# Urgent K and V of two input blocks, one VectorE key tile in the first run, and a stricter limit for TensorE's filling work

## The chip, the cores and the metric

The kernel runs on one core of a Trainium2 chip. The metric is the device time of one execution in microseconds (us). Single executions of one and the same kernel lie up to 10 us apart here, so most comparisons below rest on five or more executions a kernel, taken in three batches, each on one chip in turn with the kernel before, and name the mean granted clock of TensorE (PE).

## The reference

```python
def reference(A_x, A_wqkv, A_wo, B_x, B_w1, B_b1, B_w2, B_b2, c, w_mod):
    # x is 1 x 2048 x 512, 32 heads of 16, F = 1376, all bf16
    mod = (silu(c) @ w_mod).reshape(1, 6, 1, 512)       # sa, ca, ga, sb, cb, gb
    h = layernorm(x) * (1 + ca) + sa
    q, k, v = split_heads(h @ wqkv)
    x = x + ga * (merge(softmax(q @ k.T * 16 ** -0.5) @ v) @ wo)
    h = layernorm(x) * (1 + cb) + sb
    return x + gb * (gelu(h @ w1 + b1) @ w2 + b2)
```

## The kernel before: the parts that matter

The program is written by a list scheduler that runs when the kernel is built. Every operation is an object with an engine, an assumed duration, dependencies and a priority; the scheduler keeps a clock for each engine and emits the instructions in the order that it arrives at. The order is fixed from then on. On the chip each engine works its list in order and waits on semaphores.

The work is cut into 32 runs of 512 queries and four heads. A run has 16 key tiles of 128 keys, and a key tile has four units of 128x512 scores. ScalarE turns units into exp, two or three in an instruction. VectorE takes some key tiles with an integer form of exp: one conversion a unit, then four shifted copies a key tile. All products with V of one run add up in one accumulator, `od`, which has a single buffer and is copied to SBUF when the run ends. That copy, "the first OD copy", marks the end of run 0 below.

```python
OVER = 0.1                        # how much later than an exp's need a filler may end
HEAT = 1.3                        # us of PE work in 3.4 us below which passes of zeros are filled in
...
DKS = (2, 6, 10, 14)              # key tiles of a run that VectorE may take
FIRST_D, D_TIME = 1, 8.0          # from run 1 on
own = [[kt for kt in range(NT) if r < FIRST_D or kt not in DKS] for r in range(NR)]
shared = [[kt for kt in DKS if r >= FIRST_D] for r in range(NR)]
...
def ahead(self, can):             # what PE may start now
    q = [(s, o) for s, o in can if o.kind == "qkA"]
    if not q:
        return can
    limit = max(q[0][0], self.need() - q[0][1].us - PEL - 0.02) + OVER
    keep = []
    for s, o in can:
        end = s + o.us + (0.107 if o.mode[0] != "qk" else 0.0)
        if o.kind == "qkA" or end <= limit:
            keep.append((s, o))
    return keep
...
for b in range(NQ):               # the four input blocks: LN, transpose, modulate, Q, K, V
    kind = f"in{b}"
    if b < 2:
        urgent.add(kind)
    ... layer_norm(..., ("DVE", "DVE", "ACT", "ACT"), ...)
    make_k(b, 0, kind, r_ax, "ACT")
    make_v(b, 0, kind, ...)
...
    while ended:                  # when a run has ended
        ...
        urgent.add("in3")
```

The softmax here doesn't subtract the row's maximum and nothing guards it: scores larger than these inputs give would overflow.

Of the kernel before, what the change touches and what calls it, by code (L numbers as in the profile page):

```python
# [11 lines left out]
ACT = mybir.ActivationFunctionType  # L12
ALU = mybir.AluOpType
# [38 lines left out]

WIN = 3.4
PEL = 0.24
OVER = 0.1
DVE_PE = 0.0
DL = 0.14
DPL = 0.08
# [45 lines left out]
class Plan:  # L104
# [51 lines left out]
    def ahead(self, can):  # L156
# [6 lines that stand above are left out]
# [88 lines left out]
def kernel(  # L251
# [14 lines left out]
    nc = tc.nc  # L266
    P = 128
# [4 lines left out]
    NT = S // P  # L272
    QB = 512
    NQ = S // QB
    TPB = QB // P
# [6 lines left out]
    DKS = (2, 6, 10, 14)  # L282
# [4 lines left out]
    POOL_US, POOL_MIN = 0.68, 0.5  # L287
    A_US = {1: 0.49, 2: 0.92, 3: 1.345}
    PSUM_F = 4
    FIRST_D, D_TIME = 1, 8.0  # L290

    psum = bass.MemoryType.PSUM
    const = ctx.enter_context(tc.tile_pool(name="const", bufs=1))
# [7 lines left out]
    def res(name, n, shape, dt, pool=work):  # L301
        return Res(name, n, lambda i: pool.tile(shape, dt, name=f"{name}{i}"))
# [3 lines left out]
    r_st = [res(f"st{n}", 1, [P, n * QB], FP32, ps) for n in SPAN]  # L306
    r_od = res("od", 1, [P, QB], FP32, pp)
    r_ax = res("ax", 2, [P, QB], FP32, pp)
# [27 lines left out]
    urgent = set()  # L336
# [38 lines left out]
    def op(eng, *a, **k):  # L375
        o = Op(eng, *a, **k)
        if eng == "PE":
            o.due = due_now[0]
            due_now[0] += due_now[1]
        return plan.add(o)  # L380
# [30 lines left out]
    def free(owner, deps):  # L411
        return op("POOL", None, 0.0, deps, lat=0.0, prio=0.0, rel=(owner,))
# [38 lines left out]
    qmask = const.tile([P, 2], FP32, name="qmask")  # L451
# [55 lines left out]
    o_mask = op("DVE", mask, 0.4, (o_io,), prio=0.0)  # L507
# [129 lines left out]
    o_k = {}  # L637
# [5 lines left out]
    def proj(b, w, cc, kind, acq, after=None):  # L643
        return chain([(lambda ps, j=j: nc.tensor.matmul(  # L644
            out=ps[:, 0:QB], lhsT=w.tile[:, j, cc * P:(cc + 1) * P], rhs=o_h[b].tile[:, j, :],
            start=(j == 0), stop=(j == NC - 1)), MM) for j in range(NC)],
            [w, after] + o_hd[b], kind, acq, (o_h[b], w))

    def make_k(b, cc, kind, acq, eng):
        mm = proj(b, o_w[1], cc, kind, acq)  # L650
        o_k[(cc, b)] = op(eng, lambda o: copy(eng, kT[cc][b], mm.tile[:, 0:QB]), 0.6 if eng == 'DVE' else 0.5, (mm,), prio=0.3,
                          rel=(mm,))

    def make_q(b, cc, kind, acq):
        qm = op("POOL", None, 0.0, (), lat=0.0, prio=0.0, acq=r_qm)
        mm = proj(b, o_w[0], cc, kind, acq, after=qm)
        ev = op("DVE", lambda o: nc.vector.tensor_tensor(
            out=qm.tile, in0=mm.tile[:, 0:QB].unsqueeze(1).to_broadcast([P, 2, QB]),
            in1=qmask.unsqueeze(2).to_broadcast([P, 2, QB]), op=ALU.mult), 1.14, (mm, qm, o_mask),
            prio=0.3, rel=(mm,))  # L660
        evs = [ev, ev]
        o_q[(cc, b)] = (qm, evs)
        qm.uses += 1
        q_left[(cc, b)] = 8 * NT

    def make_v(b, cc, kind, acq, eng):
        def vt(ps, t):
            for j in range(NC):
                nc.tensor.matmul(out=ps[:, t * P:(t + 1) * P],  # L669
                                 lhsT=o_h[b].tile[:, j, t * P:(t + 1) * P],  # L670
                                 rhs=o_w[2].tile[:, j, cc * P:(cc + 1) * P],
                                 start=(j == 0), stop=(j == NC - 1))
        mm = chain([(lambda ps, t=t: vt(ps, t), 4 * 0.071) for t in range(TPB)],
                   [o_w[2]] + o_hd[b], kind, acq, (o_h[b], o_w[2]))

        def ev(o):
            dst = VEB[b][:, :, 8 * cc * VW:8 * (cc + 1) * VW].rearrange(
                "p t (h w) -> p t h w", w=VW)
            copy(eng, dst[:, :, :, 0:16], mm.tile[:, 0:QB].rearrange("p (t h d) -> p t h d", t=TPB, h=8))
        got = [op(eng, ev, 0.6, (mm, o_v0[b]), prio=0.3, rel=(mm,))]  # L680
        for t in DKS:
            if t // TPB == b:
                def scale(o, t=t):
                    for ph in range(1, NPH):
                        nc.gpsimd.tensor_scalar(  # L685
                            out=v_cols(VX[(t, ph)])[:, 8 * cc:8 * cc + 8, 0:16],
                            in0=v_cols(v_tile(t, 0))[:, 8 * cc:8 * cc + 8, 0:16], scalar1=PH_W[ph],
                            scalar2=0.0, op0=ALU.mult, op1=ALU.add)
                got.append(op("POOL", scale, 4 * 0.3, (got[0], o_v0[b]), prio=1.0, port=True))
        o_v[(cc, b)] = got  # L690
# [6 lines left out]
    NR = len(runs)  # L697
# [3 lines left out]
    def run_heads(r):  # L701
        b, u = runs[r]
        return (u % NC, None, u // NC) if b == LAST else (u // 2, u % 2, None)



    own = [[kt for kt in range(NT) if r < FIRST_D or kt not in DKS] for r in range(NR)]
    shared = [[kt for kt in DKS if r >= FIRST_D] for r in range(NR)]
    at = {"A": [0, 0, 3], "D": [0, 0, []]}
    turn = [0]  # L710

# [42 lines left out]
    def qk_deps(r, kt):  # L754
        want_q(r // 2 + 1 if r < LAST * 8 else r - LAST * 4 + 2)
        cc, par, hb = run_heads(r)
        qm, evs = o_q[(cc, runs[r][0])]
        return [evs[0], o_k[(cc, kt // TPB)]], qm

    def qk_a():  # L760
        got = []
# [16 lines left out]
        for r, kt, i in got:  # L778
            d, qm = qk_deps(r, kt)
            deps += d  # L780
            if qm not in rel:
                rel.append(qm)
# [28 lines left out]
    def qk_d():  # L811
# [10 lines left out]
        ph = o_ph[0]  # L822
        live["D"] += 1
        deps, qm = qk_deps(r, kt)
        last = len(rows) == 1

# [423 lines left out]
    prev_tr = after = None  # L1250
    for b in range(NQ):
        kind = f"in{b}"
        if b < 2:
            urgent.add(kind)
        o_h[b], o_hd[b], za, trs = layer_norm(
            lambda t, b=b: o_x[b].tile[:, t, :], o_x0 if b == 0 else [o_x[b]] * TPB, modA, o_mA, prev_tr, r_blk,
            ("DVE", "DVE", "ACT", "ACT"), tuple(r_st) if b == 0 else (r_ax, r_ax), kind, 0.6 + 0.2 * b, after)
        prev_tr = trs[-1]
        after = za[-1]
        o_h[b].uses += 1  # L1260
        free(o_x[b], za)
        if b == 0:
            make_q(0, 0, kind, r_st[0])
        make_k(b, 0, kind, r_ax, "ACT")
        make_v(b, 0, kind, r_st[1] if b == 0 else r_ax, "DVE")
# [14 lines left out]
    def want_q(g):  # L1280
        while q_made[0] < g and q_made[0] + 1 < NQ * NC:
            q_made[0] += 1
            b, cc = divmod(q_made[0], NC)
            due(32 + APR * (first_run(q_made[0]) - 1) - 32)
            make_q(b, cc, f"q{q_made[0]}", r_ax)
            due(1e9)
            if cc == NC - 1:
                o_h[b].uses -= 1
                if b == NQ - 1:
                    o_w[0].uses -= 1  # L1290
# [4 lines left out]
    while True:  # L1295
# [7 lines left out]
        while ended:  # L1303
            r = ended.pop(0)
            if r < NR - 1:
                normalise(r)
            b, u = runs[r]
# [72 lines left out]
```

## Time and profile before

| | kernel before |
|---|---|
| median of 3 executions | 813.59 us (811.69 to 815.46) |
| span of the profiled execution | 810.6 us |
| mean granted clock in it | 0.984 |
| ScalarE, VectorE, PE busy | 769.6, 737.2, 749.0 us |
| first exp, first OD copy, end of the last exp | 17.99, 60.56, 785.27 us |

An L with a number is a line of the program (from L662 on, the changed kernel's numbers are 4 higher, from L1255 on 3). In a line of the timeline, the first number is the start, the second the time to the end of the last of xN instructions, and the brackets hold the engine's idle time ahead of it and what ended that. In a line of the busy time in stretches, each engine has its busy time and, in brackets, its instructions; then come the granted clock, the share of the DMA engines and GB/s. The lines themselves stand in the prediction.

### The profile page before, as it was taken

What the parts mean: (1) busy time and instruction counts of PE and PEld (TensorE: products, weight loads), DVE (VectorE), ACT (ScalarE), POOL (GpSimd) and SP (SyncE); (2) the same over time, 40 slices, a digit from 0 to 9 for tenths busy, and PEclk for the clock granted to TensorE, in tenths of its full rate; (3) what the DMA queues carried; (4) which work ended last, traced back from release to release, by engine and by line L of the source; (5) the groups of instructions that cost most, each with busy time, mean ns of one, the idle gap of its engine ahead of it and who ended that gap; (6) DMA issues with size and microseconds to landing.
All of it is one profiled execution on the core that took longest, in us unless ns stands there. A gap on an engine that the chain in (4) does not pass through costs nothing. (4 is left out here: it accounts for less than half of the span.)

```text
span 810.6 us, 20166 instructions
## 1 busy us (share of the span) xinstructions
PE 749.0 (92%) x8217; PEld 280.3 (35%) x8217; DVE 737.2 (91%) x1281; ACT 769.6 (95%) x694; POOL 96.7 (12%) x241
## 2 busy tenths in 40 slices
PE   7889999999989999989999889989999999999997
PEld 3433333332223223223223223323234444444454
DVE  7728997989999999997899999999999999989994
ACT  2899999999999999999999999999999999999994
POOL 5321302100001100000001100000000110101100
PEclk8999999999999999989999999999999999999999
DMA  6304000002100000001110000000011001000010
GB/s 208 105 1 125 28 18 16 20 27 70 40 19 15 16 18 15 13 8 30 32 39 12 22 6 16 18 16 21 29 38 19 17 18 43 18 22 25 18 43 27
DMA packets 34199, 26.22 MB, mean 32 GB/s; under 512 B 15005, under 2 KB 29502, under 8 KB 34106
## 3 DMA queue, kind: packets, MB, share of 16 engines
q1 hardware_dynamic: 33578, 24.94, 11.0%
q8 instruction: 64, 1.05, 0.6%
q14 instruction: 29, 0.24, 0.1%
q10 hardware_dynamic: 528, 0.00, 0.0%
HBM read 21.30 MB, written 2.61 MB: 29 GB/s over the span
## 5 line engine op out<-in xcount | busy, mean ns | idle before, releaser
L798 ACT ACTIVATE pt<-st 128x1536 bf16<-128x1536 f32 x635 | 725.1, 1282 | 11.3 <-PE st L749 8.1
L839 DVE TENSOR_SCALAR ph<-ax 128x512 int16<-128x512 f32 x460 | 300.1, 684 | 20.2 <-PE ax L749 18.2
L854 DVE TENSOR_SCALAR sh<-ph 128x2048 int16<-128x2048 int16 x460 | 300.8, 694 | 4.8 <-PE od L887 4.4
L749 PE MATMUL st<-qm,kT 32*128 32x512 bf16 x1588 | 249.9, 384 | 32.6 <-ACT pt L798 26.2
L749 PEld LDWEIGHTS <-kT 32*128 32x128 bf16 x2048 | 86.0, 91 | 265.7 <-issue 255.8
L749 PE MATMUL ax<-qm,kT 32*128 32x512 bf16 x460 | 162.0, 382 | 7.9 <-DVE ph L839 5.7
L887 PE MATMUL od<-sh,VX 128*32 128x512 bf16 (+1 forms) x2320 | 162.4, 341 | 5.0 <-DVE sh L854 4.2
L887 PE MATMUL od<-pt,VEB 128*32 128x512 bf16 (+1 forms) x1980 | 151.2, 342 | 0.9 <-ACT pt L798 0.4
L887 PEld LDWEIGHTS <-VEB 128*32 128x32 bf16 x2560 | 65.3, 96 | 77.5 <-issue 61.9
L887 PEld LDWEIGHTS <-VX 128*32 128x32 bf16 x2320 | 57.1, 95 | 78.8 <-issue 67.7
L939 POOL TENSOR_TENSOR OT<-OD,RB 128x256 bf16<-128x256 f32 x38 | 28.4, 757 | 306.1 <-DVE sh L854 174.7
L887 PE MATMUL od<-ph,VEB 128*32 128x512 bf16 (+1 forms) x580 | 47.8, 341 | 2.7 <-DVE OD L912 1.8
L939 POOL TENSOR_TENSOR OS<-OD,RB 128x256 bf16<-128x256 f32 x24 | 17.1, 728 | 200.9 <-DVE sh L854 161.7
L644 PE MATMUL ax<-blk,w 128*128 128x512 bf16 x124 | 37.0, 390 | 2.6 <-ACT blk L575 1.6
L1102 PE MATMUL ax<-blk,W 128*128 128x512 bf16 (+1 forms) x148 | 38.1, 370 | 0.4 <-DVE ph L839 0.2
L1039 PE MATMUL ax<-w,g 128*128 128x512 bf16 x112 | 32.1, 410 | 0.0
L685 POOL TENSOR_SCALAR VX<-VEB 128x128 bf16<-128x128 bf16 x64 | 22.8, 357 | 77.0 <-DVE VEB L585 73.3
L1112 DVE TENSOR_SCALAR g<-ax,b1c 128x512 bf16<-128x512 f32 (+1 forms) x37 | 26.5, 718 | 0.0
L912 DVE COPY OD<-od 128x512 f32<-128x512 f32 x31 | 21.2, 684 | 3.3 <-issue 2.7
L559 DVE BATCH_NORM_STATS2 ln_s<-xb 128x6 f32<-128x512 bf16 x32 | 21.8, 681 | 1.8 <-DMA xb<-in_A_x_dram 1.7
L1039 PEld LDWEIGHTS <-g 128*128 128x128 bf16 x176 | 15.1, 100 | 23.1 <-issue 12.6
L585 DVE CAST VEB<-ax 128x512 bf16<-128x512 f32 x15 | 10.2, 680 | 12.8 <-PE ax L669 12.8
(109 smaller groups left out, 377.5 us busy)
## 6 DMA issues: line engine op xcount, KB each, us to landing
RB<-rn SPq DMA_DIRECT2D x124, 64.0 KB
xb<-in_A_x_dram SPq DMA_DIRECT2D x8, 512.0 KB
out_dram<-o SPq DMA_DIRECT2D x16, 128.0 KB
w<-in_A_wqkv_dram SPq DMA_DIRECT2D x3, 512.0 KB
W<-in_B_w_dram SPq DMA_DIRECT2D x1, 1376.0 KB
blk<-in_w_mod_dram SPq DMA_DIRECT2D x2, 512.0 KB
g<-in_w_mod_dram SPq DMA_DIRECT2D x2, 512.0 KB
xb<-in_w_mod_dram SPq DMA_DIRECT2D x2, 512.0 KB
```

The lines of the kernel that those rows point to most:

```text
L559: nc.vector.bn_stats(out=st6, in_=src)
L644: return chain([(lambda ps, j=j: nc.tensor.matmul(out=ps[:, 0:QB], lhsT=w.tile[:, j, cc * P:(cc + 1) * P], rhs=o_h[b].tile[:, j, :], start ...
L685: nc.gpsimd.tensor_scalar(out=v_cols(VX[(t, ph)])[:, 8 * cc:8 * cc + 8, 0:16], in0=v_cols(v_tile(t, 0))[:, 8 * cc:8 * cc + 8, 0:16], scala ...
L749: nc.tensor.matmul(out=o.tile[:, k * QB:(k + 1) * QB], lhsT=kT[cc][kb][rows, ko * P:(ko + 1) * P], rhs=qm.tile[rows, par, :] if hb is None ...
L798: nc.scalar.activation(out=e.tile[:, 0:len(got) * QB], in_=o.tile[:, 0:len(got) * QB], func=ACT.Exp, scale=ESC)
L839: nc.vector.tensor_scalar(out=ph.tile[:, o.row * QB:(o.row + 1) * QB], in0=o.tile, scalar1=PH_B, scalar2=0.0, op0=ALU.add, op1=ALU.max)
L854: sh = op("DVE", lambda o, j=j: nc.vector.tensor_scalar(out=o.tile, in0=first.tile, scalar1=PH_SH[j], scalar2=None, op0=ALU.add), 0.6, es, ...
L887: nc.tensor.matmul(out=o_od[r].tile[32 * i:32 * i + 32, n * HB:n * HB + w], lhsT=v_tile(kt, ph)[:, c0:c0 + 32], rhs=got[i][:, at:at + w], ...
L939: two = [op("POOL", lambda o, c=c: after_dve(nc.gpsimd.tensor_tensor(out=OT.tile[:, c * HB:(c + 1) * HB], in0=OD.tile[:, c * HB:(c + 1) * HB],
L1039: nc.tensor.matmul(out=ps, lhsT=g[:, f, col:col + P], rhs=rhs, start=(f == 0), stop=(f == NF - 1))
L1102: mm = chain([(lambda ps, f=f, j=j: nc.tensor.matmul(out=ps[:, 0:N], lhsT=W1[:, j, f * P:(f + 1) * P], rhs=h.tile[:, j, 0:N], start=(j == ...
L1112: ev.append(op("DVE", lambda o, f=f, mm=mm: nc.vector.tensor_scalar(out=g.tile[:, f, 0:N], in0=mm.tile[:, 0:N], scalar1=b1c[:, f:f + 1], s ...
```

## The change

The intent is to let ScalarE and VectorE leave run 0 sooner. LN, K and V of the third and fourth block become urgent on PE from the start, VectorE does all of the fourth block's modulation and key tile 14 of run 0, and the first Q comes in two halves. A filler on PE may no longer end later than an exp needs its scores.

```diff
-OVER = 0.1
+OVER = 0.0
...
-    FIRST_D, D_TIME = 1, 8.0
+    FIRST_DKS, D_TIME = (14,), 8.0
...
-        ev = op("DVE", lambda o: nc.vector.tensor_tensor(
-            out=qm.tile, in0=mm.tile[:, 0:QB].unsqueeze(1).to_broadcast([P, 2, QB]),
-            in1=qmask.unsqueeze(2).to_broadcast([P, 2, QB]), op=ALU.mult), 1.14, (mm, qm, o_mask),
-            prio=0.3, rel=(mm,))
-        evs = [ev, ev]
+        if (b, cc) == (0, 0):
+            evs = [op("DVE", lambda o, p=p: nc.vector.tensor_scalar(
+                out=qm.tile[:, p, :], in0=mm.tile[:, 0:QB], scalar1=qmask[:, p:p + 1], scalar2=None,
+                op0=ALU.mult), 0.6, (mm, qm, o_mask), prio=0.1 if p == 0 else 0.45, rel=(mm,)) for p in range(2)]
+        else:
+            ...                                     # one tensor_tensor, as before
...
-    own = [[kt for kt in range(NT) if r < FIRST_D or kt not in DKS] for r in range(NR)]
-    shared = [[kt for kt in DKS if r >= FIRST_D] for r in range(NR)]
+    shared = [[kt for kt in (DKS if r else FIRST_DKS)] for r in range(NR)]
+    own = [[kt for kt in range(NT) if kt not in shared[r]] for r in range(NR)]
...
-        return [evs[0], o_k[(cc, kt // TPB)]], qm
+        return [evs[par or 0], o_k[(cc, kt // TPB)]], qm
...
-        if b < 2:
-            urgent.add(kind)
+        urgent.add(kind)
...
-            ("DVE", "DVE", "ACT", "ACT"), ...
+            ("DVE", "DVE", "ACT", "ACT") if b < 3 else ("DVE",) * 4, ...
```

More of the change, by code (lines that the diff above doesn't have):

```diff
@@ L656, in make_q @@
         mm = proj(b, o_w[0], cc, kind, acq, after=qm)
-        ev = op("DVE", lambda o: nc.vector.tensor_tensor(
-            out=qm.tile, in0=mm.tile[:, 0:QB].unsqueeze(1).to_broadcast([P, 2, QB]),
-            in1=qmask.unsqueeze(2).to_broadcast([P, 2, QB]), op=ALU.mult), 1.14, (mm, qm, o_mask),
-            prio=0.3, rel=(mm,))
-        evs = [ev, ev]
+        if (b, cc) == (0, 0):
[3 more added lines that the diff above has]
+        else:
+            evs = 2 * [op("DVE", lambda o: nc.vector.tensor_tensor(
+                out=qm.tile, in0=mm.tile[:, 0:QB].unsqueeze(1).to_broadcast([P, 2, QB]),
+                in1=qmask.unsqueeze(2).to_broadcast([P, 2, QB]), op=ALU.mult), 1.14, (mm, qm, o_mask),
+                prio=0.3, rel=(mm,))]
         o_q[(cc, b)] = (qm, evs)
@@ L1252 @@
         kind = f"in{b}"
-        if b < 2:
-            urgent.add(kind)
+        urgent.add(kind)
         o_h[b], o_hd[b], za, trs = layer_norm(
             lambda t, b=b: o_x[b].tile[:, t, :], o_x0 if b == 0 else [o_x[b]] * TPB, modA, o_mA, prev_tr, r_blk,
-            ("DVE", "DVE", "ACT", "ACT"), tuple(r_st) if b == 0 else (r_ax, r_ax), kind, 0.6 + 0.2 * b, after)
+            ("DVE", "DVE", "ACT", "ACT") if b < 3 else ("DVE",) * 4, tuple(r_st) if b == 0 else (r_ax, r_ax), kind, 0.6 + 0.2 * b, after)
         prev_tr = trs[-1]
```

## The prediction

> **What bounds the kernel now.** The change touches one scheduling stage and one global rule, so I read first the page's busy shares, then the busy time in stretches, then the timeline of ScalarE in the stretch of run 0, then the waits there. A run is one pass of attention: 512 queries, four heads, sixteen key tiles of 128 keys, 64 units of 128x512 scores. There are 32 runs. ScalarE takes units with exp (two or three in one instruction), VectorE takes up to four key tiles of a run with an integer approximation of exp.
>
> ```profile
> PE 749.0 (92%) x8217; PEld 280.3 (35%) x8217; DVE 737.2 (91%) x1281; ACT 769.6 (95%) x694; POOL 96.7 (12%) x241
> L798 ACT ACTIVATE pt<-st 128x1536 bf16<-128x1536 f32 x635 | 725.1, 1282 | 11.3 <-PE st L749 8.1
> L839 DVE TENSOR_SCALAR ph<-ax 128x512 int16<-128x512 f32 x460 | 300.1, 684 | 20.2 <-PE ax L749 18.2
> L854 DVE TENSOR_SCALAR sh<-ph 128x2048 int16<-128x2048 int16 x460 | 300.8, 694 | 4.8 <-PE od L887 4.4
> ```
>
> ScalarE carries the most (769.6 us of 810.6). Its exps alone are 725.1 us for 2048 - 460 = 1588 units, 0.457 us a unit. VectorE does its 460 units (115 key tiles) with one conversion each and four shifts a key tile; both kinds start about 0.60 us apart. So the bound is the pair, fed by PE. The exps split into two stages with different limits, and the busy time in stretches shows where ScalarE is not full:
>
> ```profile
> 18.00:58.50 40.50, 32.93 (x299) 15.67 (x297) 20.43 (x46) 35.31 (x35) 13.69 (x38) 1.00 0.17 53
> 60.00:785.00 725.00, 679.09 (x7630) 243.19 (x7628) 690.21 (x1174) 716.07 (x618) 72.66 (x120) 0.99 0.10 27
> ```
>
> The columns are the stretch, its length, then PE, weight loads, VectorE, ScalarE and GpSimd. From 60 to 785 us ScalarE idles 8.9 us in 725. In run 0 (18 to 58.5 us) it idles 5.2 us in 40.5, and VectorE is busy only 20.4. The timeline of ScalarE says why:
>
> ```profile
> 17.99 7.03 ACT L798 ACTIVATE pt<-st 128x1536 bf16<-128x1536 f32 x6 [0.87 <-PE st L749]
> 25.36 1.45 ACT L575 ACTIVATE blk<-ax,modA 128x512 bf16<-128x512 bf16 x2 [0.34 <-PE ax L607]
> 27.92 0.59 ACT L583 CAST kT<-ax 128x512 bf16<-128x512 f32 x1 [1.11 <-PE ax L644]
> 28.99 6.89 ACT L798 ACTIVATE pt<-st 128x1536 bf16<-128x1536 f32 x6 [0.48 <-PE st L749]
> 35.71 1.49 ACT L575 ACTIVATE blk<-ax,modA 128x512 bf16<-128x512 bf16 x2
> 38.31 0.58 ACT L583 CAST kT<-ax 128x512 bf16<-128x512 f32 x1 [1.11 <-PE ax L644]
> 39.43 6.88 ACT L798 ACTIVATE pt<-st 128x1536 bf16<-128x1536 f32 x6 [0.54 <-PE st L749]
> 46.15 1.49 ACT L575 ACTIVATE blk<-ax,modA 128x512 bf16<-128x512 bf16 x2
> 47.47 1.51 ACT L798 ACTIVATE pt<-st 128x1536 bf16<-128x1536 f32 x1
> 50.00 0.59 ACT L583 CAST kT<-ax 128x512 bf16<-128x512 f32 x1 [1.02 <-PE ax L644]
> ```
>
> Each of the four input blocks supplies four key tiles, about 7 us of exp, and then ScalarE runs dry until LN, transpose, modulation, K product and K copy of the next block are through. It does half of the modulation and the K copy itself. VectorE's z of the fourth block is finished at 36.4 us, yet its first transposes start at 42.17: PE could have served it earlier, but in the present code the third and fourth block are ordinary fillers until run 0 ends. VectorE's first converted score starts at 57.19 us, when ScalarE enters run 1; from 37.1 to 57.2 us it has some 4.5 us of work.
>
> **What the Trainium skill says.** "ScalarE: Activation LUTs", section What ACT_TABLE_LOAD costs, gives 186 ns + 0.833 ns an element for an ACTIVATE with immediates, with some 93 ns of overlap back to back. That is an estimate of 1.37 us for 1536 columns and 0.95 for 1024. The exp starts in the trace are 1.33 and 0.90 us apart where nothing waits, slightly better, so a unit costs 0.45 us and I use the trace. "VectorE: DVE Perf Modes", section Why PSUM operands drop a tier, says that an fp32 PSUM source runs at 1x. The trace agrees: Q's masked product, 128x1024 from PSUM in one instruction, takes 1.19 us, and a 128x512 copy from PSUM 0.69, so splitting Q in two does not make it cheaper. "TensorE: Matmul & The Clock Gate", section The HAM clock gate, describes half rate after an idle window of about 3.4 us. The trace has half-rate stretches of 3.4 or 6.8 us near 10, 222, 290, 359 and 543 us and at the very end, and ScalarE's larger waits lie beside four of them (1.18 at 224, 0.80 at 293, 1.70 at 365, 1.56 at 547 us).
>
> **The change part by part.**
> (1) Blocks three and four urgent from the start. z of the third block is ready at 29.7 us, its transposes now run at 31.7 and 34.3. If they go first, ScalarE's modulation fits between exps of the second block and K is copied by about 36.5, when those exps end. That removes most of 1.11 + 0.54 us. For the fourth block it removes 1.02 + 0.54 us. Together 3.2 us; I count 2.5, since VectorE's z and the two ax buffers also bind. The waits in front of the second block (0.34 + 1.11 + 0.48) stay: it was urgent before.
> (2) Modulation of the fourth block by VectorE alone: ScalarE loses two ACTIVATEs, 1.45 us. VectorE gains two of 0.53 us in time that is idle.
> (3) Key tile 14 of run 0 by VectorE: ScalarE loses four units, 4 x 0.45 = 1.8 us. VectorE gains 4 conversions and 4 shifts, 8 x 0.60 = 4.8 us. PE gains four more PV passes of 4 matmuls. K of the fourth block should be there by 42, so the tile ends at 47 to 50 us, while ScalarE is still in run 0: hidden.
> (4) Q of the first group in two halves: the first QK needs one half, 0.6 us earlier. But the first QK at 17.55 us follows the K copy of 16.54 to 17.12, not Q, which ended at 16.5. Worth 0 to 0.3; I count 0.
> (5) The limit for fillers, from 0.1 us after to the moment an exp needs its QK. I compared the distance of successive exp starts with the two undisturbed distances, from 75 to 780 us: 86 exps come 0.02 to 0.25 us late, together 9.9 us, and the larger gaps sum to 11.1 us. The first kind is what this rule can touch. But PE is 94% busy there (679 of 725 us), so the filler withheld comes back, and VectorE's own QK counts as filler too. I count 2 us of ScalarE time, worth some 1.5 at the end: by the rates 1/0.45 and 1/1.2 units a microsecond ScalarE is 73% of the pair.
> Sum of the first three: 2.5 + 1.45 + 1.8 = 5.7 us by which ScalarE, and with it VectorE's entry, reaches run 1 earlier. As 31 runs of unchanged work follow, nearly all of it should arrive at the end. I take off 0.7 us, because the filler products of later heads that were done in run 0's gaps are pushed into the full stretch. So 5.0 + 1.5 = 6.5 us, 813.6 - 6.5 = **807.1 us**, 0.8%.
>
> **Rivals.** (a) VectorE's LN and not PE's order holds K back. For: z of the fourth block waited for the transposes of the third (0.64 us at 35.03), and its statistics end only at 33.4. Against: 5.8 us then pass before PE starts. Then only parts 2 and 3 pay: 810 us. (b) VectorE's key tile becomes the end of run 0. The accumulator od has one buffer, so run 1's PV can't begin until the tile's last shift is multiplied; the exps would then run into full pt buffers. For: its K comes with the last block. Against: 8 x 0.60 us fit if K is there by 45. If it happens, 2 to 3 us go: 809. (c) The filler rule starves VectorE: its conversions already wait 18.2 us for QK in 29 places. PE becomes the bound and 811 to 816 is possible. (d) The rule removes most of the small lateness: 0.73 x 9.9 = 7 us more than nothing, 801. (e) The clock windows fall elsewhere: each costs about 1 to 1.7 us of ScalarE, and two more or fewer move the time by some 2 to 3 us, by chance.
>
> **Range and chances.** Run 0 gives 2.5 to 6.5 us, the rule -3 to +6, the clock and the repacked schedule about 3 either way. That makes 801 to 812.5 for 8 in 10. A gain over 2% needs 797 us, so more than run 0 and all small lateness together: 4%. A loss over 2% needs 830, which no rival gives: 1%. Within 2%: 95%.
>
> **What would show it.** Right: ScalarE goes from the second block's exps on without waits over 0.5 us, has six modulations from PSUM instead of eight, and the first OD copy (60.56 us now) starts at 54 to 56; VectorE's first conversion comes at 41 to 46 us, with 464 conversions if the later runs take as many as before. In the full stretch the late exps fall below 86. Wrong: the K copies of blocks three and four stay at 38 and 50 us (a); ScalarE or PV waits for run 0's shifts after its last exp (b); VectorE's wait for QK grows beyond 25 us (c); the shift at the first OD copy is there but is gone by 785 us.

## The result, and the profile after

The changed kernel took 805.22 us (median of 4 executions, 802.58 to 808.62) against 814.16 of the kernel before. The ratio is 0.9896, with a 95% interval of 0.9849 to 0.9943: 1% faster, inside 2%. A ratio is the mean time of one kernel's fast runs over that of the other's of the same rounds, so it is not quite the ratio of the medians. With six more executions in the last batch of experiments the changed kernel has 10, with a mean of 805.4 us; the 98 executions of the kernel before that ran beside the experiments have a mean of 813.3.

The page's busy shares, the busy time in the two stretches, and ScalarE's timeline in run 0, all of the changed kernel:

```profile
PE 733.3 (92%) x8146; PEld 273.7 (34%) x8223; DVE 742.8 (93%) x1292; ACT 763.6 (95%) x691; POOL 96.9 (12%) x241
```

```profile
18.00:58.50 40.50, 33.83 (x331) 16.20 (x334) 29.85 (x62) 37.28 (x37) 14.30 (x38) 1.00 0.11 31
60.00:785.00 725.00, 673.41 (x7595) 242.88 (x7663) 692.40 (x1185) 714.07 (x625) 73.02 (x122) 0.99 0.10 27
```

```profile
28.05 0.58 ACT L583 CAST kT<-ax 128x512 bf16<-128x512 f32 x1 [1.11 <-PE ax L644]
29.12 4.62 ACT L802 ACTIVATE pt<-st 128x1536 bf16<-128x1536 f32 x4 [0.49 <-PE st L753]
33.61 1.47 ACT L575 ACTIVATE blk<-ax,modA 128x512 bf16<-128x512 bf16 x2
34.93 1.49 ACT L802 ACTIVATE pt<-st 128x1536 bf16<-128x1536 f32 x1
36.26 0.63 ACT L583 CAST kT<-ax 128x512 bf16<-128x512 f32 x1
36.73 9.20 ACT L802 ACTIVATE pt<-st 128x1024 bf16<-128x1024 f32 x8
45.67 0.73 ACT L583 CAST kT<-ax 128x512 bf16<-128x512 f32 x1
46.95 13.66 ACT L802 ACTIVATE pt<-st 128x1024 bf16<-128x1024 f32 x12 [0.55 <-PE ax L753]
```

The K copies of the third and fourth block (36.26 and 45.67 us, before 38.31 and 50.00) come with no wait in front, and the third block's modulation fits between exps. ScalarE's busy time in run 0's stretch rises from 35.31 to 37.28 us, VectorE's from 20.43 to 29.85. The first OD copy starts at 54.88 us, 5.7 us earlier. The last exp ends at 774.73 us, 10.5 us earlier, so another 4.9 us came from the runs after it, and the tail behind the last exp took 0.7 us more. These are the profiled executions; the mean gain is 7.9 us. The profile before had two half-rate windows ahead of its first exp (10.5 to 17.3 us) and the one after had none, but the second block's K copy comes at 27.92 us before and 28.05 after, so the difference is gone by then.

The OD copy is made by VectorE, after the last product on PE. It is not the moment at which ScalarE leaves run 0. That shows in the exps on the fourth block's scores: they begin at 51.13 us before and at 46.95 after, 4.2 us earlier, and ScalarE has four units fewer to do, 1.8 us. On ScalarE's own account run 0 is therefore some 6.0 us shorter. Both marks are used below.

The account on ScalarE between its first and last exp (767.3 us before, 757.3 after) closes as follows. Four units fewer are 1.8 us. Two modulations fewer are 1.45. Lateness of exps between 75 and 780 us (the distance of successive starts above the undisturbed 1.33 and 0.90 us, from the trace's start times) fell from 21.1 to 16.3 us, 4.8. The remaining 2.0 us fit ScalarE's waits in run 0, which add up to 5.1 us before and 3.2 after. This says where ScalarE's time went, not which edit did it. That took experiments.

### The profile page after: what moved, and what is told of

Same layout as the page of the kernel before. It is cut to its first block, busy times and chain, and to the rows that moved or that the text cites. A ratio compares the mean times of both kernels' runs of the same rounds, so it can differ in the third digit from the quotient of the medians.

```text
span 800.8 us, 20101 instructions
## 1 busy us (share of the span) xinstructions
PE 733.3 (92%) x8146; PEld 273.7 (34%) x8223; DVE 742.8 (93%) x1292; ACT 763.6 (95%) x691; POOL 96.9 (12%) x241
## 5 line engine op out<-in xcount | busy, mean ns | idle before, releaser
L843 DVE TENSOR_SCALAR ph<-ax 128x512 int16<-128x512 f32 x464 | 303.0, 681 | 16.9 <-PE ax L753 15.4
L858 DVE TENSOR_SCALAR sh<-ph 128x2048 int16<-128x2048 int16 x464 | 304.5, 696 | 0.7 <-PE od L891 0.3
L753 PEld LDWEIGHTS <-kT 32*128 32x128 bf16 x2048 | 83.6, 91 | 256.0 <-issue 247.0
L891 PE MATMUL od<-pt,VEB 128*32 128x512 bf16 (+1 forms) x1976 | 147.2, 342 | 1.0 <-ACT pt L802 0.8
L891 PEld LDWEIGHTS <-VEB 128*32 128x32 bf16 x2560 | 62.1, 96 | 82.1 <-issue 69.1
L1106 PE MATMUL ax<-blk,W 128*128 128x512 bf16 (+1 forms) x128 | 34.7, 368 | 1.4 <-issue 0.5
L644 PE MATMUL ax<-blk,w 128*128 128x512 bf16 x92 | 30.8, 386 | 4.1 <-issue 1.2
L1043 PE MATMUL ax<-w,g 128*128 128x512 bf16 x102 | 28.6, 381 | 2.1 <-DVE y L1087 1.0
L1106 PEld LDWEIGHTS <-W 128*128 128x128 bf16 x176 | 14.2, 97 | 18.5 <-issue 11.4
```

Of the source, the lines that this page charges most:

```text
L644: return chain([(lambda ps, j=j: nc.tensor.matmul(out=ps[:, 0:QB], lhsT=w.tile[:, j, cc * P:(cc + 1) * P], rhs=o_h[b].tile[:, j, :], start ...
L753: nc.tensor.matmul(out=o.tile[:, k * QB:(k + 1) * QB], lhsT=kT[cc][kb][rows, ko * P:(ko + 1) * P], rhs=qm.tile[rows, par, :] if hb is None ...
L843: nc.vector.tensor_scalar(out=ph.tile[:, o.row * QB:(o.row + 1) * QB], in0=o.tile, scalar1=PH_B, scalar2=0.0, op0=ALU.add, op1=ALU.max)
L858: sh = op("DVE", lambda o, j=j: nc.vector.tensor_scalar(out=o.tile, in0=first.tile, scalar1=PH_SH[j], scalar2=None, op0=ALU.add), 0.6, es, ...
L891: nc.tensor.matmul(out=o_od[r].tile[32 * i:32 * i + 32, n * HB:n * HB + w], lhsT=v_tile(kt, ph)[:, c0:c0 + 32], rhs=got[i][:, at:at + w], ...
L1043: nc.tensor.matmul(out=ps, lhsT=g[:, f, col:col + P], rhs=rhs, start=(f == 0), stop=(f == NF - 1))
```

## The experiments

The windows in the tables are the half-rate windows of PE's clock. The trace records them in multiples of 3.41 us, and the mean granted clock gives their number in every execution: (1 - clock) x 2 x span / 3.41. For the kernel before that is (1 - 0.9847) x 2 x 813 / 3.41 = 7.3 on the mean of its 98 executions. For the changed kernel it is 6.0 on the mean of 10.

I fitted straight lines to the 236 fast executions of the table below, with a level of its own for each kernel and one slope for all: each window more goes with 0.96 us more time (standard error 0.04). The lines do not tell whether a window causes the time or goes with it. They give an estimate of how far two kernels lie apart at equal numbers of windows, with a standard error of 0.3 to 0.6 us; it is called "at equal windows" below. The changed kernel is 7.9 us faster than the kernel before on the mean and 6.6 us at equal windows.

Theory A gives the filler rule a share of its own in the gain; theory B lays what was gained after run 0 to the clock windows.

### Each part alone, and all but the filler rule

**over_only**: the kernel before with this edit alone.

```diff
-OVER = 0.1
+OVER = 0.0
```

> The kernel before with the filler limit at 0.0 and nothing else. Theory A (the rule has a share of its own): ScalarE's small lateness falls from 9.9 us (86 exps between 75 and 780 us) to about 7 us (some 66 exps, as in the changed kernel), and the time falls by 1.5 to 3 us against the kernel before. Theory B (what the changed kernel gained after run 0 is luck of the half-rate clock windows): the time is within 1 us of the kernel before once runs of equal granted clock are compared. Both: the first OD copy stays near 60.6 us.

Measured: 815.61 us (median of 17), ratio 1.0049 (1.0031 to 1.0066), so 3 to 4 us slower than before. Its mean clock was 0.979, 10 windows. The small lateness, 0.02 to 0.25 us an exp, did fall from 9.9 to 7.2 us, as the rule intends, and larger gaps rose from 11.1 to 12.7. The first OD copy moved to 62.2 us. Theory A missed: the rule did its own job and the time rose. Theory B's statement on time holds: at equal windows the kernel is only 0.8 us slower than before, and the other 2.7 us of its mean go with 2.7 more windows. Both had the OD copy wrong.

**all_but_over**: the changed kernel with the old limit.

```diff
-OVER = 0.0
+OVER = 0.1
```

> The changed kernel with the filler limit put back to 0.1. Theory A: run 0 ends as early as in the changed kernel (first OD copy near 54.9 us), and the gain is the 5.7 us of run 0 alone, some 808.5 us; small lateness stays near 10 us. Theory B: 805 to 808 us, no slower than the changed kernel by more than 1 us at equal clock.

Measured: 803.59 us (median of 5), ratio 0.9890 (0.9870 to 0.9909), clock 0.989, 5 windows. It is not slower than the changed kernel; theory A's 808.5 missed, and it came out below theory B's range too. In the profiled execution two half-rate windows began at 19.9 us and set the second block's K copy back from 28.05 to 29.88, so its first OD copy at 56.6 us corresponds to some 54.8 at full clock (my estimate, 1.8 us taken off). Lateness between 75 and 780 us was 16.3 us, as in the changed kernel. Inside the change the filler rule is therefore worth nothing that these executions can show.

**urgent_only**: the kernel before with the urgency and the fourth block's modulation.

```diff
-        if b < 2:
-            urgent.add(kind)
+        urgent.add(kind)
-            ("DVE", "DVE", "ACT", "ACT"), ...
+            ("DVE", "DVE", "ACT", "ACT") if b < 3 else ("DVE",) * 4, ...
```

> The kernel before with only the urgency of the third and fourth block and the fourth block's modulation on VectorE. Theory A by the prediction's terms: 2.5 to 3.2 us of waits and 1.45 us of modulation leave ScalarE, the first OD copy starts near 56.3 us, and the time is 4 to 4.5 us below the kernel before. Rival (VectorE's LN holds K back, not PE's order): OD copy at 59 us and a gain of 1.5 us.

Measured: 811.46 us (median of 22), ratio 0.9979 (0.9964 to 0.9993). ScalarE's timeline of this kernel:

```profile
32.67 1.46 ACT L575 ACTIVATE blk<-ax,modA 128x512 bf16<-128x512 bf16 x2
33.99 2.39 ACT L798 ACTIVATE pt<-st 128x1024 bf16<-128x1024 f32 x2
36.22 0.63 ACT L583 CAST kT<-ax 128x512 bf16<-128x512 f32 x1
36.69 9.20 ACT L798 ACTIVATE pt<-st 128x1024 bf16<-128x1024 f32 x8
45.63 0.73 ACT L583 CAST kT<-ax 128x512 bf16<-128x512 f32 x1
46.91 9.14 ACT L798 ACTIVATE pt<-st 128x1024 bf16<-128x1024 f32 x8 [0.55 <-PE st L749]
```

K comes as early as in the changed kernel, so the rival (VectorE's LN holds K back) is out. The exps on the fourth block's scores begin at 46.91 us, 4.2 us earlier than before: on ScalarE the two parts gave what their terms said (3.95). But the first OD copy starts at 58.0 us and not at 56.3, 2.6 us earlier and not 4. The order on PE and VectorE holds it back:

```profile
54.17 1.47 PE L644 MATMUL ax<-blk,w 128*128 128x512 bf16 x6
...
56.75 0.40 PE L887 MATMUL od<-pt,VEB 128*32 128x512 bf16 x4
```

```profile
56.86 1.23 DVE L657 TENSOR_TENSOR qm<-ax,qmask 128x1024 bf16<-128x1024 f32 x1
58.00 0.68 DVE L912 COPY OD<-od 128x512 f32<-128x512 f32 x1
```

By a count of the units in the trace, ScalarE's 64 units of run 0 are done at 54.7 us; PE does filler products first, multiplies the last ones with V at 56.75, and VectorE then makes a Q before it copies. The time gained is only 1.7 us on the mean and 2.0 at equal windows: from the first OD copy to the last exp it took 725.9 us, against 724.7 before and 719.8 in the changed kernel.

**tile_only**: the kernel before with key tile 14 of run 0 on VectorE.

```diff
-    FIRST_D, D_TIME = 1, 8.0
+    FIRST_DKS, D_TIME = (14,), 8.0
-    own = [[kt for kt in range(NT) if r < FIRST_D or kt not in DKS] for r in range(NR)]
-    shared = [[kt for kt in DKS if r >= FIRST_D] for r in range(NR)]
+    shared = [[kt for kt in (DKS if r else FIRST_DKS)] for r in range(NR)]
+    own = [[kt for kt in range(NT) if kt not in shared[r]] for r in range(NR)]
```

> The kernel before with only key tile 14 of run 0 on VectorE. By the prediction's term: ScalarE loses 1.8 us, the first OD copy starts near 58.8 us, a gain of 1.8 us. Rival: with the fourth block not urgent, its K comes at 50.6 us, the tile's shifts end run 0 instead (OD copy at 59 to 61 us), and the gain is 0 to 0.5 us.

Measured: 824.25 us (median of 5), ratio 1.0133 (1.0111 to 1.0155), 11 us slower. VectorE's timeline shows how run 0 ends:

```profile
51.87 0.69 DVE L839 TENSOR_SCALAR ph<-ax 128x512 int16<-128x512 f32 x1 [2.86 <-PE ax L749]
...
55.69 3.24 DVE L854 TENSOR_SCALAR sh<-ph 128x2048 int16<-128x2048 int16 x4
...
60.05 0.67 DVE L912 COPY OD<-od 128x512 f32<-128x512 f32 x1
```

K arrives only at 50.77 us, the tile's shifts end at 58.9, and the OD copy starts at 60.05, 0.5 us earlier than before. The rival was right about run 0: without urgency the tile itself ends it, while ScalarE's 60 units are done at 57.4 us, 1.5 us before the 64 of the kernel before were, although the second block's K copy came 0.8 us later here (28.68). On time it missed too, as the loss comes later. VectorE has 452 conversions, 112 key tiles in runs 1 to 31 where the kernel before has 115, so ScalarE carries three tiles more, 12 units x 0.45 = 5.4 us. Lateness rises from 21.1 to 26.9 us. One edit in run 0 repacked the whole list.

### The clock windows

**before_hot** and **after_hot**: each filling pass of zeros issued twice, in the kernel before and in the changed one; the order of the rest is untouched.

```diff
-        for i in range(4):
+        for i in (0, 1, 2, 3) * 2:
             nc.tensor.matmul(out=o_od[r].tile[32 * i:32 * i + 32, :], lhsT=warm[:, 0:32], ...
```

> The kernel before with every filling pass of zeros into the accumulator issued twice, the order of everything else unchanged; results stay right, as zeros are added. The runs so far of the kernel before have a mean granted clock of 0.985, which is some 7 half-rate windows of 3.4 us a run, and its single runs lie about 0.6 us apart for each window. Clock theory (after run 0 the kernels differ mostly by half-rate windows): the mean clock rises to 0.990 or more and the time falls to 808 to 811 us. Rival (the lateness of exps is the schedule's own, the clock only accompanies it): the clock rises but the time stays at 813 us or more, since each doubled pass takes PE some 0.2 us.

Measured: 816.91 us (median of 14), ratio 1.0042 (1.0029 to 1.0056), clock 0.985, 7 windows. The doubling did not reduce the windows (7.1 against 7.3) and the time rose by 3.4 us, 3.6 at equal windows. So this run says nothing on what a window is worth, but it says what the doubling itself costs.

> The same doubling in the changed kernel, whose runs had a mean clock of 0.987, 6 windows. Clock theory: 802 to 804 us, and the distance to the doubled kernel before is 6 to 7 us, the part of run 0 alone plus little. Rival: 805 us or more, and the distance stays 8 to 9 us.

Measured: 806.36 us (median of 6), ratio 0.9926 (0.9900 to 0.9952), clock 0.991, 4 windows. Here the windows fell by 1.7, and the mean rose by 1.7 us. That is no evidence against windows: a doubling costs 3.6 us at equal windows in the kernel before and 3.3 here, and 1.7 windows fewer take 1.6 of that back. The distance between the doubled kernels' means, 816.7 and 807.1 us, is 9.5 us and not 6 to 7, but the doubled kernels are 2.7 windows apart; at equal windows the distance is 6.9 us, what the clock theory said. The test was meant to take the windows from both kernels and took them from one, so it refutes neither theory.

**heat145**: the changed kernel, the scheduler told to fill in earlier.

```diff
-HEAT = 1.3
+HEAT = 1.45
```

> The changed kernel with the threshold for filling passes raised from 1.3 to 1.45 us of PE work in 3.4 us, so that the scheduler places them itself and plans around them. Clock theory: mean clock above 0.990, 801 to 804 us. Rival: no fewer windows, 805 us or slower.

Measured: 809.78 us (median of 22), ratio 0.9952 (0.9937 to 0.9967), clock 0.981, 9 windows. More filling was asked for (252 matmuls of zeros in its profile against 164), and the new order had more windows. The rival holds: 2.7 of the 4.1 us to the changed kernel go with windows, 1.5 stay at equal windows.

### What single pieces are worth inside the change

**no_qsplit**: the changed kernel with the first Q in one instruction.

```diff
-        if (b, cc) == (0, 0):
-            evs = [... two tensor_scalar ...]
-        else:
-            evs = 2 * [... one tensor_tensor ...]
+        evs = 2 * [... one tensor_tensor ...]
```

> The changed kernel with the first Q in one instruction again. By the prediction's term the split is worth 0 to 0.3 us: first exp at 17.4 to 18.0 us, first OD copy near 54.9 us, time within 1 us of the changed kernel. Rival (in the changed kernel Q was last before the first QK, as its K copy was already done at 15.3 us): first exp 0.5 us later and the time 0.5 us longer.

Measured: 804.42 us (median of 6), ratio 0.9897 (0.9871 to 0.9923); first OD copy at 54.5 us. The split is worth nothing: in the changed kernel the first exp waits for Q (2.10 us at 17.43), but ScalarE then waits for the second block's K, whose copy comes at 28.05 us with the split and at 27.69 without.

**after_again**: the changed kernel once more.

> The changed kernel once more, in the same rounds as the next three and with more runs than the four it had. Theory C (what stands after eight runs: run 0 ends 5.7 us earlier, 2 to 3 us more come from later runs that happen to be packed with less lateness of exps, and the filler rule is worth nothing inside the change): 804 to 806 us, so 7.5 to 9 us below the kernel before, and level within 1.5 us with all_but_over's 803.6. Theory A (the filler rule has a share of its own): the changed kernel comes out at 803 us or below, ahead of all_but_over.

Measured: 804.22 us (median of 6, 802.42 to 812.26), ratio 0.9896 (0.9851 to 0.9940). It agrees with the first result and with theory C's statement; it stands level with all_but_over. In its profile, which had half-rate windows at 10.3 and 20.5 us, the first OD copy came at 55.9 us.

**mod_on_act**: the changed kernel with the fourth block's modulation shared again.

```diff
-            ("DVE", "DVE", "ACT", "ACT") if b < 3 else ("DVE",) * 4, ...
+            ("DVE", "DVE", "ACT", "ACT"), ...
```

> The changed kernel with half of the fourth block's modulation back on ScalarE. Prediction's term: two ACTIVATEs, 1.45 us, come back on ScalarE in run 0, the first OD copy moves from 54.9 to some 56.3 us (clock windows in the first 20 us apart), and the time by the same, 806.5 to 807 us, unless the later runs are repacked. Rival: ScalarE has slack there and run 0 ends as before, below 55.4 us.

Measured: 814.57 us (median of 14), ratio 1.0028 (1.0001 to 1.0056), clock 0.972, 13 windows. With the two ACTIVATEs back, the whole gain is gone. ScalarE's and VectorE's timelines of this kernel:

```profile
46.88 0.73 ACT L583 CAST kT<-ax 128x512 bf16<-128x512 f32 x1
48.16 14.58 ACT L802 ACTIVATE pt<-st 128x1024 bf16<-128x1024 f32 x13 [0.55 <-PE ax L753]
```

```profile
48.14 2.49 DVE L843 TENSOR_SCALAR ph<-ax 128x512 int16<-128x512 f32 x4 [0.55 <-PE ax L753]
50.66 2.50 DVE L858 TENSOR_SCALAR sh<-ph 128x2048 int16<-128x2048 int16 x4
...
54.27 0.68 DVE L916 COPY OD<-od 128x512 f32<-128x512 f32 x1
```

On ScalarE the two ACTIVATEs do cost nearly what the prediction says: the exps on the fourth block's scores begin at 48.16 us and not at 46.95, 1.2 us later. The OD copy, at 54.27 us, is not later, because VectorE's four conversions go back to back here (2.49 us), while in the changed kernel they wait for scores and stretch from 46.93 to 50.78 us. From the OD copy to the last exp it took 726.1 us (719.8 in the changed kernel) and the tail 30.0 (26.0). The mean lies 10.2 us above the changed kernel's, with 7.3 windows more. At equal windows 3.2 us are left, or 1.9 by this kernel's own line, since few executions of the others have so many windows. So most of the loss goes with windows, and what is left is not far from the prediction's 1.45. Part of the 6.3 us is visible in the busy time of the stretches that begin with a Gelu. ScalarE loads a table, does one Gelu of 4.9 us and loads the exp table back, 7.5 us without an exp. The last two of this kernel's three:

```profile
507.50:522.50 15.00, 12.97 (x86) 3.25 (x79) 13.56 (x22) 13.15 (x9) 0.52 (x1) 0.68 0.01 3
699.00:714.00 15.00, 12.86 (x95) 3.81 (x92) 12.59 (x21) 13.12 (x9) 0.52 (x1) 0.66 0.01 3
```

All three of the kernel before, then all three of the changed kernel:

```profile
351.00:366.00 15.00, 12.76 (x72) 3.65 (x70) 13.25 (x22) 13.24 (x9) 0.52 (x1) 0.77 0.01 2
534.00:549.00 15.00, 12.93 (x94) 3.67 (x95) 12.85 (x21) 13.38 (x9) 1.93 (x3) 0.89 0.04 10
695.00:710.00 15.00, 13.78 (x210) 6.19 (x202) 14.17 (x25) 14.94 (x11) 2.17 (x3) 1.00 0.09 26
```

```profile
324.00:339.00 15.00, 12.86 (x82) 4.01 (x83) 10.82 (x19) 14.96 (x10) 0.52 (x1) 1.00 0.04 11
505.00:520.00 15.00, 13.26 (x110) 3.97 (x100) 14.85 (x25) 14.94 (x11) 1.93 (x3) 1.00 0.05 14
706.00:721.00 15.00, 13.10 (x146) 4.98 (x147) 14.93 (x29) 14.94 (x11) 4.10 (x5) 1.00 0.09 21
```

The fourth busy time is ScalarE's, the number after the brackets the clock. Where the clock stayed at 1.00, ScalarE idled 0.04 to 0.06 us in 15; where it fell to 0.66 to 0.89, 1.6 to 1.9 us. All 14 profiles taken have three such stretches each. In the 21 with a clock of 1.00 ScalarE idled at most 0.3 us, in the other 21 between 0.9 and 2.5. In the kernel before the three idle 3.4 us together, in the changed kernel 0.1. So some 3.3 of the 4.9 us that its profiled execution gained after run 0 lie in the Gelu stretches. But that is not a fixed property of the change: no_qsplit, with the changed kernel's edits but one, idled 3.2 us in them in its profile (span 806.3), and the changed kernel's second profile again 0.1 (span 801.3).

### Going further

**two_tiles**: the changed kernel with two key tiles of run 0.

```diff
-    FIRST_DKS, D_TIME = (14,), 8.0
+    FIRST_DKS, D_TIME = (10, 14), 8.0
```

> The changed kernel with key tiles 10 and 14 of run 0 on VectorE. ScalarE loses another 1.8 us. If VectorE's 6.5 us of idle time between its last z and its first conversion are really free: first OD copy at 53 us and 803 us. If the same thing happens as in tile_only (a second tile makes VectorE's shifts the end of run 0, or the later runs lose VectorE tiles): first OD copy at 54.5 us or later, VectorE tiles in later runs below 115, and 806 to 811 us.

Measured: 808.17 us (median of 12, the slow one included), ratio 0.9923 (0.9899 to 0.9948), clock 0.980. One execution of 1179 us, with a clock of 1.00, is marked slow on record and left out of the ratio; nothing on record explains it. VectorE took only one tile in run 0 after all, since ScalarE may take a shared tile back when it runs out of its own; in later runs VectorE had 114 tiles. The profiled execution had four half-rate windows from 20.1 us, so its first OD copy (60.4 us) can't be compared. The rival's range was hit, but not by a second tile: the kernel had 9.3 windows, and at equal windows it is level with the changed kernel.

**retuned**: five constants of the scheduler moved, chosen by letting the scheduler alone compare a few hundred combinations.

```diff
-OVER = 0.0
+OVER = 0.05
-    FIRST_DKS, D_TIME = (14,), 8.0
+    FIRST_DKS, D_TIME = (14,), 7.0
-    TAIL, CB = 185, 49
-    TAIL2, TAIL3 = 148, 95
+    TAIL, CB = 185, 55
+    TAIL2, TAIL3 = 140, 95
-            ... d_run() <= a_run[0] + (a_run[0] > 3)
+            ... d_run() <= a_run[0] + (a_run[0] > 1)
```

> The changed kernel with five constants of the scheduler moved that do not touch run 0's sequence on purpose: filler limit 0.05, the waiting time of VectorE's look-ahead 7, the pace of the tails and of later K and V, and look-ahead from run 2 on. If the later stretch is a matter of how the list schedule happens to pack (theory C), this can be better than the changed kernel by 1 to 4 us with run 0 unchanged: 801 to 804 us, VectorE tiles in later runs 115 or more. If the stretch is bound by the engines: 804 to 806 us.

Measured: 804.11 us (median of 6, lowest 799.66), ratio 0.9866 (0.9832 to 0.9900), 116 VectorE tiles in later runs. The interval overlaps that of the changed kernel in the same rounds (0.9851 to 0.9940), so it is not shown to be better. At equal windows it is 3.7 us better; its windows, 7.8 against 6.0, take part of that back.

| kernel | executions | median us | windows, mean | first OD copy us | VectorE tiles, runs 1 to 31 | us from before, at equal windows |
|---|---|---|---|---|---|---|
| before | 98 | 812.75 to 813.70 in three batches | 7.3 | 60.6 | 115 | 0 |
| changed | 4 and 6 | 805.22, 804.22 | 6.0 | 54.9, 55.9 | 115 | -6.6 |
| over_only | 17 | 815.61 | 10.0 | 62.2 | 114 | +0.8 |
| all_but_over | 5 | 803.59 | 5.1 | 56.6 (two windows in run 0) | 115 | -7.5 |
| urgent_only | 22 | 811.46 | 7.5 | 58.0 | 115 | -2.0 |
| tile_only | 5 | 824.25 | 8.4 | 60.0 | 112 | +8.9 |
| before_hot | 14 | 816.91 | 7.1 | 60.7 | 115 | +3.6 |
| after_hot | 6 | 806.36 | 4.3 | 55.6 | 115 | -3.3 |
| heat145 | 22 | 809.78 | 8.8 | 56.0 | 115 | -5.2 |
| no_qsplit | 6 | 804.42 | 6.1 | 54.5 | 115 | -7.4 |
| mod_on_act | 14 | 814.57 | 13.3 | 54.3 | 115 | -3.4 |
| two_tiles | 11 of 12 | 808.17 | 9.3 | 60.4 (four windows in run 0) | 114 | -7.2 |
| retuned | 6 | 804.11 | 7.8 | 55.2 | 116 | -10.3 |

## Why the prediction was right, and which steps were not

The time (807.1 predicted, 805.4 measured as the mean of 10) and the range held. The step that carried it is confirmed: ScalarE leaves run 0 some 6 us earlier (5.7 predicted), and in this order of the program it reaches the end. That is no rule: in urgent_only ScalarE was 4.2 us ahead, and 2.0 us at equal windows arrived. The terms of run 0 hold one by one when they are read on ScalarE, the engine that they speak of. That the OD copy moved by the same 5.7 us is in part chance, as the order on PE and VectorE moves it too. The term of the filler rule failed, and its 1.5 us were made up by luck: 1.3 windows fewer, which the prediction did not count.

- **Part 1, urgency, 2.5 us.** Confirmed: the waits of 1.11, 0.54 and 1.02 us are gone in urgent_only and in the changed kernel, 2.7 us; the last 0.54, after the fourth block's K copy, stays (0.55). K of the fourth block came later than I wrote, at 45.67 us and not by 42. VectorE's first conversion came at 46.93, outside the 41 to 46 that I named, and the tile's shifts ended at 53.5 and not by 50.
- **Part 2, modulation, 1.45 us.** Confirmed on ScalarE: mod_on_act gave it back, and the exps on the fourth block's scores began 1.2 us later. The OD copy did not show it.
- **Parts 1 and 2 together, 3.95 us.** Urgency with modulation brought those exps forward by 4.2 us (51.13 to 46.91). The OD copy moved by 2.6 (60.6 to 58.0).
- **Part 3, key tile, 1.8 us.** On ScalarE it is four units fewer, as counted: its share of run 0 is done at 52.5 us, against 54.7 in urgent_only (in steps of two or three units). On the OD copy it depends on part 1: 0.5 us alone, some 3.1 on top of urgency (58.0 to 54.9, with a Q split that no_qsplit shows to be worth nothing). It is 3.1 and not 1.8 because the OD copy of urgent_only was held back.
- **Part 4, Q in halves, 0.** Confirmed.
- **Part 5, the filler rule, 1.5 us.** This is the term that failed. Alone it costs 3 to 4 us, 0.8 at equal windows, and inside the change it is worth nothing. The small lateness does fall, as I counted, but other gaps and windows take its place.
- **Rival (b)**, the tile as the end of run 0, is what happens without urgency. **Rival (c)**, a starved VectorE, did not come about: its conversions' wait for scores fell from 18.2 us to 15.4 in the changed kernel.
- **Rival (e)**, the clock, was named with the wrong origin. I called it chance of 2 to 3 us. Within one kernel it is close to that: over the changed kernel's first four executions, 802.6 us at a clock of 0.992 and 808.6 at 0.980, about 1 us a window. But the mean number of windows differs between orders, from 4 to 13, and so belongs to the schedule too.
- **A misreading.** From 37.1 to 57.2 us VectorE had 3.8 us of work and not 4.5. It changes no term.

What the prediction left out is how far an edit moves everything after run 0. The mean gain of 7.9 us is 6.6 at equal windows, which is near what run 0 gave, and 1.3 that go with 1.3 fewer windows; that difference has a standard error of 0.7 windows. Of the large losses, most of mod_on_act's goes with windows, and tile_only's does not: it lost VectorE tiles and gained lateness. So theory B (windows) fits the later gain as well as theory C (the packing of later runs) does, and no run decides between them. What stays open is why one order keeps PE's clock up across the Gelus and another doesn't, and whether a window causes an exp's lateness or goes with it. The doubled passes were to tell that, and they did not reduce the windows in the kernel before.

## What to carry to other kernels

When a build-time list scheduler orders the program, an edit's first-order effect (here the end of run 0) can be read off the profile and predicted, but every edit also repacks all that follows; measure a neutral edit to know that scatter before crediting a percent to a rule. Test parts in both directions, alone and as the one missing: the key tile lost 11 us alone. Read the end of a stage on the engine that the prediction speaks of: the OD copy, on another engine, hid 1.2 us that ScalarE had lost. And note the granted clock of every execution: before two kernels are compared, ask how far apart they are at equal numbers of half-rate windows.

## What the Trainium skill lacked or had wrong

- "TensorE: Matmul & The Clock Gate", section The HAM clock gate, says that the gate follows how busy PE has been and falls to half rate after an idle window of about 3.4 us. It has no threshold for how much work counts as idle, and the trace's busy time does not give one. In the changed kernel PE was busy 2.92 us of the 3.41 before 423.38 us, where the clock fell, and only 2.41 us of the 3.41 from 324.39 us on, after which it stayed at 1.00. (Longer stretches that hold half-rate time are no use for this, as the matmuls in them are drawn out: 0.63 us for one of 128x512 in the window at 10.5 us of the kernel before, 0.38 at full rate.)
- The same page, section HAM oscillation, works out the loss for a kernel whose PE waits for DMA. I found no page that has what goes with a window in a kernel that is bound by ScalarE: 0.96 us a 3.4 us window between executions of one program, and 0.9 to 2.5 us of ScalarE in a Gelu stretch with one to three windows.
- "ScalarE: Activation LUTs", section What ACT_TABLE_LOAD costs: its figures for ACTIVATEs with immediates give an estimate of 1.47 us for one of 1536 columns and of 1.37 us from start to start, as it has back-to-back ones overlap by some 93 ns. Here, with the scores in PSUM, an exp of 1536 columns takes 1.45 us and the starts are 1.33 us apart, so the overlap is about 0.12 us.
